# Gathering the output in two tiles of two groups by turns instead of one tile of four groups

## The chip, the cores and the metric

One core of one Trainium2 chip runs the whole program. The metric is the device time of one launch in microseconds. Three runs of the kernel before gave 1164.0, 1164.9 and 1166.22 us; the median is 1164.9 us.

## The reference

The input `x` has 4 batches of 12608 rows with 128 columns, and there are 32 inducing rows. Two attention steps follow each other (`mab`): first the inducing rows attend over all of `x` and give 32 rows `h` per batch, then every row of `x` attends over `h`. On that result stands a channel mix in the manner of RWKV: each row is mixed with the row before it, once for a key path of width 1024 and once for a gate.

```python
def mab(q, kv):
    s = scale * (q @ kv.T); a = exp(s - s.max(-1)); a /= a.sum(-1) + 1e-09
    return a @ kv
h = mab(I, x);  x = mab(x, h)
x_prev = x shifted by one row (a zero row first)
xk = mu_k * x + (1 - mu_k) * x_prev ;  xr = mu_r * x + (1 - mu_r) * x_prev
k = maximum(xk @ w_k, 0);  v = k * k @ w_v;  r = sigmoid(xr @ w_r)
return r * v            # (4, 12608, 128) float32
```

## The kernel before

**Tiles.** A batch is cut into 25 groups of 512 rows (the last has 320), and a group into 4 units; a unit is a quarter of the 1024 inner columns. The program is one long list of 400 units, written out by hand: the order in which the instructions of each engine stand is the order of the calls in the loop over `n` at the end, and no scheduler moves them.

**One unit.** `up` (L779, L781) multiplies the attention weights of the group, which lie in a tile `R`, by products `W` of `h` with the weights, 4 matmuls on TensorE (PE) into the accumulator `ps_a`. `square` takes that apart: VectorE (DVE) writes the positive part to `k_t` (L791), ScalarE (ACT) or DVE squares it into a high part `kh` (L796, L793), ACT squares it once more in full (L797), and GpSimd (POOL) takes the difference, the low part `kl` (L799). Four units later (`LAG`) `down` adds `kh`·`wvh`, `kh`·`wvl` and `kl`·`wvh` into `ps_v`, 6 matmuls (L810).

**The end of a group.** After the last unit of a group has been through `down`, `gate` multiplies by the sigmoid on DVE into `oT` (L815), and `store` transposes `oT` in blocks of 32 by 32 on DVE into the output tile `ot` (L826). `store` of group g of a batch is called at unit 4g+9 of that batch, ahead of that unit's `down` and of what is due there. `ot` has one buffer (`bufs=1`) of 4 groups. After the fourth group four DMAs, one for each 32 partitions, take it to memory (L833), 256 KB each. The next group's transpose (the first of the next four) writes the same buffer, and so it has to wait until all four have landed. The last four full groups of the last batch are stored one by one, and the group of 320 rows goes through another tile, `aT`. Before the first group the buffer of `ot` also holds the weights `wv_sb` while they are split into a high and a low part.

**Work for the next batch beside it.** `stage_a` transposes blocks of `x` on DVE (L333, from `xb` to `xs`) for the next batch, in segments of 12 units; four sets of four DMAs (L336) carry the pieces to the tiles `xt`, and 6 units after the last set is due PE multiplies them with the inducing rows (`scores`, L361). Then DVE takes the maximum (L364, L370), PE spreads it (L371), ACT takes exponentials, DVE transposes them (L405), and PE sums (L426). `stage_b` computes the attention weights of later groups, a high and a low part (`ah`, L656, and `al`, L660), and for each group a copy of one column from the group before (L593) and four DMAs (L670) put them into its `R`.

**One queue.** All these DMAs, but for three loads at the start, are issued by SyncE (SP) in the order of the calls. SP does one after the other: an entry that waits for its data holds up all that stand behind it.

Of the kernel before, what the change touches and what calls it, by code (L numbers as in the profile page):

```python
# [8 lines left out]
F32 = mybir.dt.float32  # L9
# [10 lines left out]
def kernel(  # L20
# [12 lines left out]
    B, N, C = x.shape  # L33
    M = inducing.shape[0]
    F = w_k.shape[1]
    P = 128
    Q = 4
    FC = F // P
    G = 512
    BLK = Q * G  # L40
    NBLK = (N + BLK - 1) // BLK
    TAIL = N - (NBLK - 1) * BLK
    WF = F + C
    UC = 2
    LAG = 4
    NU = FC // UC
    assert NBLK == 7 and C == P and M * Q == P and F % 1024 == 0 and TAIL % Q == 0
    scale = 1.0 / float(C) ** 0.5
# [8 lines left out]
    mp = ctx.enter_context(tc.tile_pool(name="mp", bufs=2))  # L57
# [19 lines left out]
    nc.scalar.dma_start(out=mur, in_=mu_r.rearrange("(p o) -> p o", o=1))  # L77
    wk_sb = const.tile([P, F], F32, name="wk_sb")
    wr_sb = const.tile([P, C], F32, name="wr_sb")
    wv_sb = mp.tile([P, Q * G], F32, name="ot", bufs=1)[:, :F].rearrange("p (c d) -> p c d", d=C)  # L80

    def load_weight(dst, src, n, raw):

# [666 lines left out]
    NG = (NBLK - 1) * Q + 1  # L750
    UB = NG * NU

    class Group:
# [63 lines left out]
        def store(self):  # L817

            g, w = self.g, self.w
            if g == NG - 1:  # L820
                self.S.ot = st.tile([P, G], F32, name="aT")
            elif g % Q == 0:
                self.S.ot = out_tile()
            ot = self.S.ot
            o = (g % Q) * G
            nc.vector.transpose(out=ot[:, o:o + w], in_=self.oT)  # L826
            span = 1 if self.b == B - 1 and g // Q == NBLK - 2 else Q
            if g % span == span - 1 or g == NG - 1:
                o0 = (g % Q - g % span) * G
                t0 = (g - g % span) * G  # L830
                dst = out[self.b, t0:t0 + o - o0 + w, :].rearrange("(s q) (j d) -> j q s d", q=M, d=M)
                for i in range(Q):
                    nc.sync.dma_start(out=dst[i], in_=ot[M * i:M * (i + 1), o0:o + w]  # L833
                                      .rearrange("q (s d) -> q s d", d=M))

    def out_tile():
        return mp.tile([P, Q * G], F32, name="ot", bufs=1)


    def run(th):  # L840
# [107 lines left out]
    def start():  # L948

        sc0, df0, ex0, nm0, pl0 = stage_b_head([0, 1])  # L950
        sc1, df1, ex1, nm1, pl1 = stage_b_head([2, 3])
        hi0, lo0, put0 = pl0[0]
        box = {}

        def bank():
            return pv.tile([P, G], F32, name="ps_v")

        def gate_bank(s):
            if s == 0:
                box["g"] = bank()  # L960
            return box["g"][:, s * C:(s + 1) * C]

        wa = [wpart(s, 0, bank) for s in range(2)]
        wb = [wpart(s, 1, bank) for s in range(2)]
        wg = [wpart(s, None, lambda s=s: gate_bank(s)) for s in range(2)]
        assert F // G == 2
        hi1, lo1, put1 = pl0[1]
        run([sc0, lambda: halo(batches[0], 0), df0, wa[0][0], wa[1][0], wa[0][1], ex0, wa[1][1], wa[0][2], nm0, wb[0][0], hi0, lo0, put0,
             wa[1][2], wb[0][1], hi1, lo1, wb[0][2]])
        at(0, mixed_r)  # L970
        for f in (wb[1][0], wb[1][1]):
            soon(0, f)
        for n, f in ((0, wb[1][2]), (0, sc1), (1, df1), (1, ex1), (2, nm1)):
            at(n, f)
        for prod, high, low in wg:
            at(1, prod)
        for prod, high, low in wg:
            at(1, high)
            at(2, low)
        soon(2, put1)  # L980
        for k, (high, low, put) in enumerate(pl1):
            at(k + 2, high)
            at(k + 3, low)
            at(k + 5, put)
        at(4, lambda: units[0][0].zgate(first=True))
# [16 lines left out]
    for b in range(B):  # L1002
        for g in range(NG):
            grp = Group(b, g)
            units += [(grp, u) for u in range(NU)]
    end = len(units) - 1
    late = []
    with tc.manual_schedule():
        head()
        start()  # L1010
        for n in range(len(units) + LAG + 2):
            grp, u = units[n] if n < len(units) else (None, n % NU)
            old, ou = units[n - LAG] if LAG <= n < len(units) + LAG else (None, 0)
            m = n - LAG - 1
            if 0 <= m < len(units) and units[m][1] == NU - 1:
                units[m][0].gate()
# [3 lines left out]
            else:  # L1020
# [9 lines left out]
                if n == end:  # L1030
                    run(late)
                    late = []
                if n >= NU and u == 1:
                    grp.zgate()
                if u == NU - 2 and n + 2 < len(units):
                    nxt = units[n + 2][0]
# [37 lines left out]
```

## Time and profile before

| | |
|---|---|
| median of 3 runs | 1164.9 us |
| the profiled execution | 1164.7 us |
| its span, first to last instruction | 1162.9 us |
| outside the span | 1.8 us |
| mean granted TensorE clock | 0.993 |
| PE busy | 1117.1 us |
| POOL busy | 947.7 us |
| DVE busy | 933.2 us |

All are from one profiled execution except the median. A row of the waits names the instruction that waited, what ended the wait, the total in us, how often, and the longest. A row of the timeline has the start and the duration in us, the engine (SPq is SP's queue issuing a DMA), the line, the operation, output and input, how many were merged into the row, and in brackets the idle time of that engine just before it with what ended it. The duration of an SPq row is the time in which the queue was taken up with issuing, not the transfer.

### The profile page before, as it was taken

The numbers are of one execution on the slowest core, as the hardware profiler recorded it, in microseconds if no ns is written. First come the engines' busy times: TensorE is split into PE (matmuls) and PEld (weight loads), VectorE is DVE, ScalarE is ACT, GpSimd is POOL, SyncE is SP. The second block draws the span as 40 slices with busy tenths as digits, with TensorE's granted clock in tenths as the row PEclk, the third lists the DMA queues.
The fourth block names the chain that finished last, engine by engine and source line by source line (L and its number), as shares of the span: only waits on it lengthen the run. The fifth ranks groups of instructions, "written<-read, shape, count | busy, mean of one in ns | idle before, by whom it ended". The sixth has DMA issues, their size and how long they took to land.

```text
span 1162.9 us, 17578 instructions
## 1 busy us (share of the span) xinstructions
PE 1117.1 (96%) x5746; PEld 836.6 (72%) x5746; DVE 933.2 (80%) x1259; ACT 970.9 (83%) x1107; POOL 947.7 (81%) x413
## 2 busy tenths in 40 slices
PE   6789999999999999999999999999999999999997
PEld 4466777776677777777768777677768777777886
DVE  5788888886878888888787889897787888877665
ACT  5488888887888888788978988888789888889996
POOL 1168888887787888888879888878878899999997
PEclk9999999999999999999999999999999999999999
DMA  9122654544226355465043553645204314432231
GB/s 295 42 50 64 130 120 112 102 117 81 44 56 134 105 106 123 108 133 120 5 77 77 117 124 105 133 98 122 45 18 79 63 34 73 73 64 46 43 46 34
DMA packets 273515, 102.31 MB, mean 88 GB/s; under 512 B 232816, under 2 KB 248336, under 8 KB 271120
## 3 DMA queue, kind: packets, MB, share of 16 engines
q1 hardware_dynamic: 273088, 101.17, 40.7%
q8 instruction: 46, 0.75, 0.3%
q14 instruction: 45, 0.37, 0.1%
q10 hardware_dynamic: 336, 0.02, 0.0%
HBM read 28.07 MB, written 25.82 MB: 46 GB/s over the span
## 4 chain that ended last, share of the span: by engine, by line
PE 65%; DVE 13%; ACT 8%; issue 5%; DMA 4%; SPq 4%; POOL 0%; DVEq 0%; ACTq 0%; POOLq 0%
PE ps_v L810 33%; PE ps_a L779 12%; PE ps_a L781 11%; DVE k_t L791 5%; ACT kh L796 2%; DMA out_dram<-ot 2%; PE pb_a L426 2%; ACT k_t L797 2%; PE ps_v L768 1%; SPq L833 1%; PE pb_b L616 1%; PE ps_v L769 1%; PE pb_a L361 1%; ACT L771 1%; ACT L633 1%
## 5 line engine op out<-in xcount | busy, mean ns | idle before, releaser
L799 POOL TENSOR_TENSOR kl<-k_t,kh 128x1024 fp32r<-128x1024 f32 (+2 forms) x400 | 939.0, 2375 | 175.8 <-ACT k_t L797 156.5
L791 DVE TENSOR_SCALAR k_t<-ps_a 128x1024 f32<-128x1024 f32 (+1 forms) x400 | 480.7, 1202 | 154.3 <-PE ps_a L781 143.5
L797 ACT ACTIVATE k_t<-k_t 128x1024 f32<-128x1024 f32 (+1 forms) x400 | 418.2, 1048 | 45.5 <-DVE kh L793 34.3
L796 ACT ACTIVATE kh<-k_t 128x1024 fp32r<-128x1024 f32 (+1 forms) x352 | 366.0, 1040 | 106.7 <-DVE k_t L791 56.1
L779 PE MATMUL ps_a<-R,W 128*128 128x512 f32 (+1 forms) x800 | 326.3, 408 | 6.7 <-DMA R<-al 3.4
L781 PE MATMUL ps_a<-R,W 128*128 128x512 f32 (+1 forms) x800 | 314.2, 393 | 0.0
L810 PE MATMUL ps_v<-kh,wvh 128*128 128x512 f32 (+1 forms) x800 | 252.2, 396 | 5.6 <-ACT rT L771 5.2
L810 PE MATMUL ps_v<-kh,wvl 128*128 128x512 f32 (+1 forms) x800 | 250.1, 394 | 0.0
L810 PE MATMUL ps_v<-kl,wvh 128*128 128x512 f32 (+1 forms) x800 | 250.0, 394 | 0.0
L779 PEld LDWEIGHTS ps_a<-R,W 128*128 128x128 f32 x800 | 151.4, 189 | 84.8 <-issue 20.7
L810 PEld LDWEIGHTS ps_v<-kh,wvh 128*128 128x128 f32 x800 | 147.9, 189 | 42.4 <-ACT rT L771 10.2
L810 PEld LDWEIGHTS ps_v<-kl,wvh 128*128 128x128 f32 x800 | 150.4, 189 | 35.8 <-POOL kl L799 0.3
L810 PEld LDWEIGHTS ps_v<-kh,wvl 128*128 128x128 f32 x800 | 150.3, 189 | 35.0
L781 PEld LDWEIGHTS ps_a<-R,W 128*128 128x128 f32 x800 | 151.3, 189 | 29.9
L826 DVE STREAM_TRANSPOSE ot<-oT 128x512 f32<-128x512 f32 x96 | 67.4, 702 | 12.0 <-DMA out_dram<-ot 11.2
L815 DVE TENSOR_TENSOR oT<-ps_v,rT 128x512 f32<-128x512 f32 (+1 forms) x100 | 66.6, 666 | 2.4 <-PE ps_v L810 0.2
L793 DVE SCALAR_TENSOR_TENSOR kh<-ps_a,k_t 128x1024 fp32r<-128x1024 f32 x48 | 58.8, 1225 | 5.4 <-PE ps_v L810 0.5
L771 ACT ACTIVATE rT<-ps_v 128x512 f32<-128x512 f32 (+1 forms) x99 | 57.3, 579 | 0.3
L333 DVE STREAM_TRANSPOSE xs<-xb 128x512 f32<-128x512 f32 x72 | 50.0, 694 | 1.8 <-DMA xb<-in_x_dram 1.6
L771 ACT ACT_TABLE_LOAD x31 | 39.8, 1283 | 0.6
L768 PE MATMUL ps_v<-R,W 128*128 128x512 f32 (+1 forms) x99 | 39.1, 395 | 0.1
L769 PE MATMUL ps_v<-R,W 128*128 128x512 f32 (+1 forms) x99 | 38.7, 391 | 0.0
(192 smaller groups left out, 642.3 us busy)
## 6 DMA issues: line engine op xcount, KB each, us to landing
out_dram<-ot SPq DMA_DIRECT2D x92, 256.0 KB, 4.3
xb<-in_x_dram SPq DMA_DIRECT2D x18, 1024.0 KB, 5.3
xt<-xs SPq DMA_DIRECT2D x288, 64.0 KB, 2.0
R<-ah SPq DMA_DIRECT2D x184, 64.0 KB, 2.0
R<-al SPq DMA_DIRECT2D x184, 64.0 KB, 2.0
kh<-in_x_dram SPq DMA_DIRECT2D x4, 512.0 KB, 7.0
kl<-in_x_dram SPq DMA_DIRECT2D x4, 512.0 KB, 6.3
xb<-in_x_dram SPq DMA_DIRECT2D x8, 256.0 KB, 5.5
```

Source lines behind the costliest of these rows:

```text
L768: nc.tensor.matmul(out=ps[:, :w], lhsT=S.W[0][:, F:WF], rhs=R[:, 1:w + 1], start=True, stop=False)
L771: nc.scalar.activation(out=self.rT, in_=ps[:, :w], func=AF.Sigmoid)
L779: nc.tensor.matmul(out=ps[:, c, :w], lhsT=S.W[0][:, cs], rhs=R[:, 1:w + 1], start=True, stop=False)
L781: nc.tensor.matmul(out=ps[:, c, :w], lhsT=S.W[1][:, cs], rhs=R[:, 0:w], start=False, stop=True)
L791: nc.vector.tensor_scalar(out=k, in0=self.ps[:, :, :w], scalar1=0.0, scalar2=None, op0=ALU.max)
L793: nc.vector.scalar_tensor_tensor(out=kh, in0=self.ps[:, :, :w], scalar=0.0, in1=k, op0=ALU.max, op1=ALU.mult)
L796: nc.scalar.activation(out=kh, in_=k, func=AF.Square)
L797: nc.scalar.activation(out=k, in_=k, func=AF.Square)
L799: return lambda eng, a, z: eng.tensor_tensor(out=kl[:, :, a:z], in0=k[:, :, a:z], in1=kh.bitcast(F32)[:, :, a:z], op=ALU.subtract)
L810: nc.tensor.matmul(out=self.v, lhsT=wt[:, fc, :], rhs=kk[:, c, :], start=(fc == 0 and n == 0), stop=(fc == FC - 1 and n == 2))
L815: nc.vector.tensor_tensor(out=self.oT, in0=self.v, in1=self.rT, op=ALU.mult)
L826: nc.vector.transpose(out=ot[:, o:o + w], in_=self.oT)
```

## The change

A constant `UO = 2` is added. The tile `ot` holds `UO` groups instead of four, and its pool keeps its two buffers (the pool's default), so that the bytes in SBUF stay the same. `store` takes a new tile at every even group, and issues its four DMAs after every odd group, 128 KB each instead of 256 KB. The helper `out_tile` goes away. The one-by-one stores of the last four full groups of the last batch and the last group of each batch stay as they are.

```diff
+    UO = 2
...
-    wv_sb = mp.tile([P, Q * G], F32, name="ot", bufs=1)[:, :F].rearrange("p (c d) -> p c d", d=C)
+    wv_sb = mp.tile([P, UO * G], F32, name="ot")[:, :F].rearrange("p (c d) -> p c d", d=C)
...
-            elif g % Q == 0:
-                self.S.ot = out_tile()
+            elif g % UO == 0:
+                self.S.ot = mp.tile([P, UO * G], F32, name="ot")
             ot = self.S.ot
-            o = (g % Q) * G
+            o = (g % UO) * G
             nc.vector.transpose(out=ot[:, o:o + w], in_=self.oT)
-            span = 1 if self.b == B - 1 and g // Q == NBLK - 2 else Q
+            span = 1 if self.b == B - 1 and g // Q == NBLK - 2 else UO
             if g % span == span - 1 or g == NG - 1:
-                o0 = (g % Q - g % span) * G
+                o0 = (g % UO - g % span) * G
                 t0 = (g - g % span) * G
                 dst = out[self.b, t0:t0 + o - o0 + w, :].rearrange("(s q) (j d) -> j q s d", q=M, d=M)
                 for i in range(Q):
                     nc.sync.dma_start(out=dst[i], in_=ot[M * i:M * (i + 1), o0:o + w]
                                       .rearrange("q (s d) -> q s d", d=M))
-
-    def out_tile():
-        return mp.tile([P, Q * G], F32, name="ot", bufs=1)
```

In the order of the instructions PE, DVE, ACT and POOL keep every row in its place, a row's line number apart. What differs there is what some of them wait for. The first place is DVE at the end of the fifth group of the first batch, where a transpose turns to a new output buffer; before (DMAHW0 to DMAHW7 are the eight semaphores by which DMAs report that they have landed, taken by turns; Pool, PE, Activation and DVE are those of the engines):

```order
L791 TENSOR_SCALAR k_t<-ps_a 128x1024 [waits PE_49,Pool_49]
L826 STREAM_TRANSPOSE ot<-oT 128x512 [waits DMAHW2_49,DMAHW7_49,DMAHW1_49,DMAHW0_49]
L364 TENSOR_REDUCE mx_1487<-pb_a 128x1 [waits PE_49]
L791 TENSOR_SCALAR k_t<-ps_a 128x1024 [waits PE_49,Pool_49]
L660 TENSOR_TENSOR al<-pb_b,ah 128x512 [waits DMAHW6_49,DMAHW5_49,Activation_49]
```

The same place in the changed kernel, where lines stand one further down:

```order
L792 TENSOR_SCALAR k_t<-ps_a 128x1024 [waits PE_49,Pool_49]
L827 STREAM_TRANSPOSE ot<-oT 128x512 [waits DMAHW3_49]
L365 TENSOR_REDUCE mx_1492<-pb_a 128x1 [waits PE_49]
L792 TENSOR_SCALAR k_t<-ps_a 128x1024 [waits PE_49,Pool_49]
L661 TENSOR_TENSOR al<-pb_b,ah 128x512 [waits DMAHW4_49,DMAHW3_49,DMAHW5_49,DMAHW2_49,DMAHW6_49,DMAHW1_49,Activation_49]
```

The transpose waits for the four stores of the block that has just ended before, and afterwards for a store of groups 0 and 1, whose buffer it takes over; no row has moved.

On SP the stores move. This is its queue at the start of the first batch, ahead of the attention weights of group 4, before:

```order
L336 DMA xt<-xs 32x512 x16
L205 DMA xb<-in_x_dram 128x2048
L593 DMA R<-R 128x1
L670 DMA R<-ah 32x512
L670 DMA R<-al 32x512
```

The same stretch in the changed kernel:

```order
L337 DMA xt<-xs 32x512 x16
L206 DMA xb<-in_x_dram 128x2048
L834 DMA out_dram<-ot 32x32x32 x4
L594 DMA R<-R 128x1
L671 DMA R<-ah 32x512
```

The stores of groups 0 and 1 now stand ahead of the column copy and the four DMAs that fill the `R` of group 4.

This is SP's queue in the second segment of the second batch, from the second to the third of its four sets of `xt`, before:

```order
L336 DMA xt<-xs 32x512 x4
L593 DMA R<-R 128x1
L670 DMA R<-ah 32x512
L670 DMA R<-al 32x512
L670 DMA R<-ah 32x512
L670 DMA R<-al 32x512
L336 DMA xt<-xs 32x512 x4
```

The same stretch in the changed kernel:

```order
L337 DMA xt<-xs 32x512 x4
L834 DMA out_dram<-ot 32x32x32 x4
L594 DMA R<-R 128x1
L671 DMA R<-ah 32x512
L671 DMA R<-al 32x512
L671 DMA R<-ah 32x512
L671 DMA R<-al 32x512
L337 DMA xt<-xs 32x512 x4
```

The stores of groups 0 and 1 of the second batch stand between the two sets, where no store stood before.

## The prediction

> **What bounds the kernel now.** I read the shares of the engines and the chain that ended last first:
>
> ```profile
> PE 1117.1 (96%) x5746; PEld 836.6 (72%) x5746; DVE 933.2 (80%) x1259; ACT 970.9 (83%) x1107; POOL 947.7 (81%) x413
> PE ps_v L810 33%; PE ps_a L779 12%; PE ps_a L781 11%; DVE k_t L791 5%; ACT kh L796 2%; DMA out_dram<-ot 2%; PE pb_a L426 2%; ACT k_t L797 2%; PE ps_v L768 1%; SPq L833 1%; PE pb_b L616 1%; PE ps_v L769 1%; PE pb_a L361 1%; ACT L771 1%; ACT L633 1%
> ```
>
> PE is busy for 1117.1 of 1162.9 us, so that 45.8 us of idle PE is all that any edit of waits can bring. The chain gives the stores of `ot` 2% of the span (some 23 us), but a step of that chain lasts as long as the store, while PE beside it works on. What counts is PE's idle time. The waits of DVE, which executes the transpose, and those of PE after the first 90 us:
>
> ```profile
> DVE ot L826 <- DMA out_dram<-ot: 11.2, 6, 2.7
> DVE k_t L791 <- PE ps_a L781: 143.5, 177, 2.8
> PE pb_b L371 <- DVE mx L370: 4.0, 3, 1.8
> PE ps_a L779 <- DMA R<-al: 3.4, 2, 2.1
> PE pb_b L371 <- DVE al L660: 2.2, 3, 1.1
> PE pb_a L426 <- DVE e L405: 0.7, 1, 0.7
> ```
>
> DVE loses 11.2 us to the one output buffer, in six waits. It waits 143.5 us for PE, so it has time to spare; only what PE then waits for DVE is lost. The third, fifth and sixth row name such waits. One of the places in full, the queue, DVE and PE in turn:
>
> ```profile
> 501.93 4.54 SPq L833 DMA_DIRECT2D out_dram<-ot  x4
> 510.11 0.71 DVE L826 STREAM_TRANSPOSE ot<-oT 128x512 f32<-128x512 f32 x1 [2.43 <-DMA out_dram<-ot]
> 513.18 0.38 PE L371 MATMUL pb_b<-ident,mx 128*128 128x128 f32 x1 [0.86 <-DVE al L660]
> ```
>
> The queue issues the stores of a block from 501.93 to 506.47, they land, the next transpose starts 2.43 us late at 510.11, the DVE work behind it (L364, L660) is late too, and PE stands for 0.86 us. A wait of 2.43 us costs 0.86.
>
> **What the change removes.** With two buffers the transpose waits for stores that were issued two groups earlier. A group takes about 11 us (100 groups in the span), far more than the stores need, so all six waits go. What PE gets back at the other places:
>
> ```profile
> 137.05 0.38 PE L371 MATMUL pb_b<-ident,mx 128*128 128x128 f32 x1 [0.26 <-DVE al L660]
> 225.21 0.32 PE L426 MATMUL pb_a<-xb,e 128*32 128x128 f32 x4 [0.73 <-DVE e L405]
> 790.94 0.38 PE L371 MATMUL pb_b<-ident,mx 128*128 128x128 f32 x1 [1.13 <-DVE al L660]
> 276.66 0.35 PE L371 MATMUL pb_b<-ident,mx 128*128 128x128 f32 x1 [1.80 <-DVE mx L370]
> 550.50 0.35 PE L371 MATMUL pb_b<-ident,mx 128*128 128x128 f32 x1 [1.14 <-DVE mx L370]
> 269.33 0.71 DVE L826 STREAM_TRANSPOSE ot<-oT 128x512 f32<-128x512 f32 x1 [2.00 <-DMA out_dram<-ot]
> ```
>
> With 0.86 the first three make 0.26 + 0.73 + 0.86 + 1.13 = **2.98 us**. Nothing else stands next in line there: PE's list of waits has no second releaser at these instructions.
>
> The stall at 276.66 is another matter. The same matmul waits 1.14 us in the next batch, where no store held DVE; so the store's part is not 1.80 but 1.80 - 1.14 = 0.66 us. Why the rest stays is seen in POOL and DVE:
>
> ```profile
> 274.13 2.37 POOL L799 TENSOR_TENSOR kl<-k_t,kh 128x1024 fp32r<-128x1024 f32 x1 [2.01 <-ACT k_t L797]
> 274.56 1.95 DVE L370 TENSOR_TENSOR mx<-mx,mx 128x1 f32<-128x1 f32 x1
> 549.08 1.27 DVE L370 TENSOR_TENSOR mx<-mx,mx 128x1 f32<-128x1 f32 x1
> 277.35:280.76 3.41, 3.41 (x10) 2.66 (x9) 0.94 (x4) 2.11 (x2) 1.48 (x1) 0.50 0.09 18
> 550.50:553.91 3.41, 3.41 (x16) 2.83 (x17) 2.13 (x5) 2.24 (x3) 2.41 (x1) 1.00 0.09 18
> ```
>
> An operation on 128 by 1 numbers takes 1.95 and 1.27 us, and in the first batch it ends at 276.51, where POOL's ends (276.50). It is held by whatever POOL is doing, and that is not touched by the change. The last two rows are windows of the trace (length, busy time of PE, its weight loads, DVE, ACT and POOL, then the clock): right after this stall PE ran for 3.41 us at a granted clock of 0.50, which loses 3.41 x 0.5 = 1.7 us. Behind the stall of 1.14 us in the next batch the clock is full. Without the store I expect 1.14 here too, and no halving: 0.66 + 1.7 = **2.36 us**.
>
> The Trainium skill ("TensorE: Matmul & The Clock Gate", "What's actually happening") says that the clock is halved by a monitor that looks at windows of 3413 ns that run on regardless of the program; the 3.41 us of the row agrees. By that rule it is chance in part whether a stall falls into one window, so that this term might be 0.66; the sum below would then be a gain of 4.4 instead of 6.1.
>
> **What it adds.** The stores rise from 124 DMAs to 216 (the 92 large DMAs of the first row below, 23 blocks of four groups, become 184; 16 of 64 KB and 16 of the last groups stay), at the same bytes and the same rows of 128 bytes. SP issues them, and the columns and the pieces of `R` and `xt` stand behind them. The trace has sets of four with 256 KB each and with 64 KB each, not with 128:
>
> ```profile
> out_dram<-ot SPq DMA_DIRECT2D x92, 256.0 KB, 4.3
> 406.66 4.24 SPq L833 DMA_DIRECT2D out_dram<-ot  x4
> 410.94 1.77 SPq L593 DMA_DIRECT2D R<-R  x1
> 395.31 0.51 SPq L593 DMA_DIRECT2D R<-R  x1
> 1140.16 1.94 SPq L833 DMA_DIRECT2D out_dram<-ot  x4
> ```
>
> A large set takes the queue 4.24 us and holds the next entry for 1.77 - 0.51 = 1.26 us more: 5.5. A set of 64 KB takes 1.94. A set of 128 KB lies between 1.94 and 5.5; by size, a third of the way, 1.94 + 3.56 / 3 = 3.1 us. I take 3.1, since issuing grows with size in these rows. Two sets then take 6.2 where one took 5.5: in sum almost nothing, but each half stands elsewhere. Where a large set stood the queue is 2.4 us earlier, and where none stood it is 3.1 us later. Two places gain and two lose.
>
> *Gain, `xt` in the fourth segments.* The scores take 1.06 us where nothing holds them, as in the row at 405.82 below; two took longer:
>
> ```profile
> 454.89 4.39 SPq L833 DMA_DIRECT2D out_dram<-ot  x4
> 470.09 2.64 SPq L336 DMA_DIRECT2D xt<-xs  x4
> 473.18 2.11 PE L361 MATMUL pb_a<-xt,indT 128*32 128x512 f32 x8
> 750.85 1.90 PE L361 MATMUL pb_a<-xt,indT 128*32 128x512 f32 x8
> 399.53 2.43 SPq L336 DMA_DIRECT2D xt<-xs  x4
> 405.82 1.06 PE L361 MATMUL pb_a<-xt,indT 128*32 128x512 f32 x8
> 674.71 3.24 SPq L336 DMA_DIRECT2D xt<-xs  x4
> 683.42 1.06 PE L361 MATMUL pb_a<-xt,indT 128*32 128x512 f32 x8
> xt<-xs SPq DMA_DIRECT2D x288, 64.0 KB, 2.0
> ```
>
> The last of the four `xt` DMAs from 470.09 is issued at about 472.2 and lands 2.0 us later, when the scores have begun. They lose 2.11 - 1.06 = 1.05 us, and 0.84 at 750.85. The queue had been late since the large set at 454.89; 2.4 us earlier, both losses go: **1.89 us**.
>
> *Loss, `xt` in the second segments.* The set from 399.53 has its last DMA issued at 399.53 + 3 x 0.62 = 401.4; it lands at 403.4, 2.4 us ahead of its use at 405.82. With 3.1 us more ahead of it PE waits **0.7 us**. Below 2.4 us the set is hidden, at 5.5 it costs 3.1. Its twin in the third batch, issued by 677.95 at the latest, lands by 679.95, 3.5 us ahead of its use at 683.42, and stays hidden.
>
> *Loss, the first `R`.*
>
> ```profile
> 96.61 0.70 DVE L826 STREAM_TRANSPOSE ot<-oT 128x512 f32<-128x512 f32 x1
> 98.21 0.52 SPq L670 DMA_DIRECT2D R<-ah  x1
> 101.25 0.51 SPq L670 DMA_DIRECT2D R<-al  x1
> 104.56 0.47 PE L779 MATMUL ps_a<-R,W 128*128 128x512 f32 x1 [1.31 <-DMA R<-al]
> ```
>
> PE waits here for the `R` of group 4 already. Its first high part went out at 98.21 and the low part at 101.25, when DVE had it. Now the queue first waits for group 1's transpose (97.31), and is free of the stores at 97.4 + 3.1 = 100.5; column and high part take 0.51 + 0.52 and two gaps, so the low part goes at 101.65: **0.4 us** late. At 1.94 it is hidden; at 5.5 it is 2.8 late. All other `R` are filled well ahead or behind a set that shrinks.
>
> Everything else is nothing: `wv_sb` gets a tile that group 2 takes over long after the weights were split, and the stores that end the last batch are the same.
>
> **The sum.** 2.98 + 2.36 + 1.89 - 0.7 - 0.4 = 6.1 us. The profiled execution took 1164.7 us (span 1162.9 and 1.8 outside), 0.2 below the median 1164.9. 1164.7 - 6.1 = **1158.6 us**.
>
> **The rivals.** *PE gets little of it.* DVE's time is gained, but the halved clock comes back at another stall, L361 stays late for reasons of its own, and only the four direct stalls go: 2.98 - 0.7 - 0.4 = 1.9 us, **1162.8 us**. For it: of DVE's 11.2 us the most is hidden as it is, and the three waits for L370 depend on where POOL is. Against it: each term has its own row with its own releaser.
>
> *Slower: the stores of half the size take the queue as long as the whole ones.* If a set of 128 KB takes 5.5 us, the second segment loses 3.1, the first `R` 2.8, and its stall of 1.31 + 2.8 = 4.1 brings a halved clock, 1.7: 7.6 in all. L361 gets no relief, so the gain is 5.34: 1164.7 + 2.3 = **1167.0 us**. It decides from about 4.9 us a set on. For it: in the large set three DMAs of four take over 1 us each. Against it: 64 KB takes 0.49 each. The Trainium skill ("DMA: Bandwidth & Descriptors", "Rules for kernel authors") speaks against the change here: many small transfers should be gathered into a large one, and under 64 KB one pays mostly overhead. At 128 KB the rule is not broken outright, and no row of this size is there to hold against it.
>
> *The change doesn't take the waits away.* The order of the instructions shows that the transpose now waits for a store of the pair before the last; so this is left at nothing.
>
> **How the numbers follow.** Forecast 0.78, little gained 0.16, slower 0.06. About 0.2% (2.3 us) is what a measurement of this kernel can tell from no change: faster is below 1162.6. The forecast's own bounds: with sets of 1.94 us both losses vanish (1157.5), and one of the three stalls before L370, or one halved clock more or less, moves it by up to 1.7 to either side: 1155.8 to 1161.4. With little gained the range reaches up to 1163.0. So 1155.8 to 1163.0, faster 0.78, same 0.16, slower 0.06.
>
> **What would show it.** In the profile after: no row of L826 waiting for a store; L371 no longer waiting for L660; the stall before L371 in the first batch near 1.1 us and full clock behind it; 216 stores in sets that take some 2 to 3 us; L361 at 1.06 us in the fourth segments, and a new wait of under 1 us in the second segment of the second batch. The forecast is wrong if PE's busy time and span stay apart by the same 45.8 us, if a halved clock shows at a new place, or if the sets take over 4.9 us.

## The result and the profile after

The changed kernel takes 1156.13 us (median of 6 runs, 1155.37 to 1159.7) where the kernel before takes 1164.45 us on the same chip (6 runs, 1162.18 to 1166.22). The ratio is 0.9936, with a 95% interval of 0.9918 to 0.9954: 8.3 us faster. The forecast was faster, by 6.1 us, to 1158.6 us; the time lies in the range, close to its lower end. The profiled execution took 1155.37 us with a span of 1153.6, that is 9.3 us less span than before.

The shares of the engines and the chain that ended last, after:

```profile
PE 1111.2 (96%) x5746; PEld 834.2 (72%) x5746; DVE 933.7 (81%) x1259; ACT 971.4 (84%) x1107; POOL 948.4 (82%) x413
PE 75%; DVE 11%; ACT 8%; issue 4%; DMA 1%; SPq 0%; DVEq 0%; ACTq 0%
```

The engines do the same work as before in a shorter span, and the step `out_dram<-ot`, 2% of the chain before, is down to a single one of 2.23 us. PE's busy time is 5.9 us less for the same instructions: its rows last longer in a stretch at half clock, of which this execution has fewer (below), and a row that waits inside, as the scores did, counts as busy. The waits of DVE and PE that answer to those of before; a row has the total, how often, and the longest:

```profile
DVE k_t L792 <- PE ps_a L782: 140.6, 180, 2.2
PE ps_a L780 <- DMA R<-al: 3.6, 2, 2.3
PE pb_b L372 <- DVE mx L371: 3.4, 3, 1.1
```

There is no row of L827 (L826 before) waiting for a store, none of PE waiting at L372 for L661 and none of PE waiting for L405. What is left is the wait for the maximum, three times 1.1 us, and the two for `R`. The place that the prediction showed in full, in the second batch, in SP's queue, DVE and PE:

```profile
495.95 2.48 SPq L834 DMA_DIRECT2D out_dram<-ot  x4
501.42 0.70 DVE L827 STREAM_TRANSPOSE ot<-oT 128x512 f32<-128x512 f32 x1
505.98 0.38 PE L372 MATMUL pb_b<-ident,mx 128*128 128x128 f32 x2
```

The rows of DVE and PE carry no bracket any more. The stores of 128 KB have left the queue at 498.43, and a store lands 2.7 us after its issue (4.3 with 256 KB), so that even a transpose into the same buffer would have found it free, at 501.1. That is the first hint that the second buffer is not what matters.

The places where the prediction expected a gain and a loss from the queue, the scores in the fourth segments and in the second segment of the second batch, with what stands in the queue ahead of them:

```profile
395.47 2.44 SPq L337 DMA_DIRECT2D xt<-xs  x4
428.89 2.48 SPq L834 DMA_DIRECT2D out_dram<-ot  x4
450.26 2.49 SPq L834 DMA_DIRECT2D out_dram<-ot  x4
461.83 2.44 SPq L337 DMA_DIRECT2D xt<-xs  x4
468.58 2.89 SPq L834 DMA_DIRECT2D out_dram<-ot  x4
```

```profile
400.91 1.07 PE L362 MATMUL pb_a<-xt,indT 128*32 128x512 f32 x8
468.03 1.06 PE L362 MATMUL pb_a<-xt,indT 128*32 128x512 f32 x8
743.49 1.07 PE L362 MATMUL pb_a<-xt,indT 128*32 128x512 f32 x8
```

All three take their undisturbed 1.06 or 1.07 us: both gains came, and the loss did not. Only the second half of the block (450.26) stands where the whole one stood, with one `xt` set between it and that of 461.83; its first half left at 428.89, and the stores of 468.58 are the first half of the next block, issued behind the last `xt` set. The 46 sets of 128 KB took the queue 2.25 to 3.59 us, 2.48 in the middle; the 23 whole ones before took 4.05 to 5.05, 4.39 in the middle. I had estimated 3.1 for the half ones.

The stall before the maximum in the first batch, the wait for the first `R` of the second batch, and the stretches of 3.41 us behind both (length, busy time of PE, PEld, DVE, ACT and POOL, the clock, the DMA share and GB/s):

```profile
273.43 0.46 PE L372 MATMUL pb_b<-ident,mx 128*128 128x128 f32 x2 [1.12 <-DVE mx L371]
339.99 0.47 PE L780 MATMUL ps_a<-R,W 128*128 128x512 f32 x1 [2.29 <-DMA R<-al]
```

```profile
273.43:276.84 3.41, 3.41 (x16) 2.83 (x17) 2.14 (x5) 2.25 (x3) 2.42 (x1) 1.00 0.02 4
341.37:344.78 3.41, 3.41 (x11) 2.92 (x10) 2.22 (x3) 2.12 (x2) 1.36 (x1) 0.50 0.35 77
```

The first stall fell from 1.80 to 1.12 us and the clock behind it is full, as forecast; the second is as before, with its halved clock. The first `R`, where I expected 0.4 us of loss:

```profile
96.15 2.29 SPq L834 DMA_DIRECT2D out_dram<-ot  x4
...
100.07 0.51 SPq L671 DMA_DIRECT2D R<-al  x1
```

```profile
103.43 0.47 PE L780 MATMUL ps_a<-R,W 128*128 128x512 f32 x1 [1.36 <-DMA R<-al]
```

1.36 us stands where 1.31 stood: nothing lost that counts.

To see where 9.3 us went I took, in both traces, the distance from the start of each matmul to the start of the next, less the usual distance of that pair of matmuls, and summed it by the place at which the matmul came late, from the eighth unit on. The levels also hold small regular delays; what counts is the difference.

| place | before | after | change | forecast |
|---|---|---|---|---|
| up to the eighth unit | 81.3 | 80.1 | -1.2 | 0 |
| scores (L361) | 9.6 | 7.7 | -1.9 | -1.89 and +0.7 |
| maximum (L371) and L426 | 18.6 | 13.7 | -4.9 | -3.64 |
| halved clock | 2.6 | 1.2 | -1.4 | -1.7 |
| late `R` (L779) | 5.1 | 5.4 | +0.3 | +0.4 |

The rest, in small pieces, is about half a us, and behind the last matmul after has 0.3 us more. The 1.2 us at the start belong to the clock, not to the change:

```profile
55.46:58.87 3.41, 3.41 (x14) 1.61 (x16) 2.83 (x5) 0.61 (x3) 0.00 (x0) 0.50 0.00 0
65.70:69.10 3.40, 3.40 (x10) 2.62 (x9) 3.24 (x7) 2.13 (x4) 2.31 (x2) 0.50 0.02 5
```

These are two stretches at half clock in the trace of before; after has only one there, at 64.90. The first two kernels of the experiments begin as the kernel before does, and their profiled executions reach the eighth unit at 80.0 and 81.2 us, with no such stretch and with two. The profiled executions of two kernels below (one buffer with half stores, and four tiles of one) spend 2 us more than before up to the eighth unit, at a mean clock of 0.992 and 0.991.

### The profile page after: what moved, and what is told of

The parts are those of the page before. It is cut to its first block, busy times and chain, and to the rows that moved or that the text cites. A ratio compares the mean times of both kernels' runs of the same rounds, so it can differ in the third digit from the quotient of the medians.

```text
span 1153.6 us, 17710 instructions
## 1 busy us (share of the span) xinstructions
PE 1111.2 (96%) x5746; PEld 834.2 (72%) x5746; DVE 933.7 (81%) x1259; ACT 971.4 (84%) x1107; POOL 948.4 (82%) x413
## 4 chain that ended last, share of the span: by engine, by line
PE 75%; DVE 11%; ACT 8%; issue 4%; DMA 1%; SPq 0%; DVEq 0%; ACTq 0%
PE ps_v L811 38%; PE ps_a L780 14%; PE ps_a L782 12%; DVE k_t L792 4%; ACT kh L797 2%; PE pb_a L427 2%; PE pb_b L617 2%; PE ps_v L769 2%; PE ps_v L770 2%; PE pb_a L362 2%; ACT k_t L798 1%; ACT L772 1%; ACT L634 1%; DVE oT L816 1%; DVE kh L794 1%
## 5 line engine op out<-in xcount | busy, mean ns | idle before, releaser
L827 DVE STREAM_TRANSPOSE ot<-oT 128x512 f32<-128x512 f32 x96 | 67.4, 702 | 0.0
```

## The experiments

My theory after the result: PE's gain comes from two sources, the wait of the transpose for its buffer, and the queue of SP, in which a whole set takes 4.4 us and the `xt` pieces stand behind it. Each is worth about what the table says. The rivals: all comes from the buffer; or all comes from the size of the sets, and the second buffer does nothing.

**The wait gone, the queue kept.** The first group of each four goes to a tile of its own, so that its transpose finds a free buffer; the stores still leave together after the fourth group, as four DMAs of 64 KB and four of 192 KB. Edit of the kernel before (its core):

```diff
-            elif g % Q == 0:
-                self.S.ot = out_tile()
...
+            if g == NG - 1 or (g % Q == 0 and not alone):
+                self.S.of = st.tile([P, G], F32, name="aT")
...
+            elif g % Q == Q - 1:
+                pieces = [(self.S.of, 0, g - 3, G), (self.S.ot, G, g - 2, 3 * G)]
```

> The buffer wait alone is taken away: the first group of four goes to the tile aT, the other three to the one tile ot, and all are stored after the fourth group, as before (eight stores at that place instead of four, 64 KB and 192 KB each, estimated at about the 5.5 us of queue time that a block takes before). My sum holds term by term: PE gets back the direct stalls (2.98 us) and the stall of the first batch with its halved clock (2.36), not the scores of the fourth segments (1.89). So about 5.3 us below before, 1159, L826 without waits for stores, L361 still near 2 us at two places. Rival, that the split of the queue's stores is what counts: no change, 1164.5. Rival, that the buffer wait is all: as the changed kernel, 1156.

Measured 1162.84 us against 1164.67 of before, ratio 0.9989 (0.9977 to 1.0001): almost nothing of the expected gain. The waits that are left, and the queue at the fourth segment of the second batch:

```profile
DVE aT L823 <- DMA out_dram<-aT: 5.5, 2, 3.4
PE pb_a L361 <- DMA xt<-xs: 1.8, 2, 1.3
```

```profile
453.76 2.24 SPq L841 DMA_DIRECT2D out_dram<-aT  x4
456.10 3.02 SPq L841 DMA_DIRECT2D out_dram<-ot  x4
459.16 1.35 SPq L593 DMA_DIRECT2D R<-R  x1
```

Of DVE's 11.2 us of waits 5.5 are left, twice, and those are of this experiment's own making: the group of 320 rows uses the tile `aT` too. The queue was taken up for 5.3 us by the eight stores, longer than by a whole set, and PE's scores now wait for `xt` with a row of their own. By the table's measure the scores are 4.8 us worse than before (14.4 against 9.6). So this kernel is not clean; the next leaves the queue alone.

**The wait alone gone.** The transpose of the first group of each four is simply called one unit (2.3 us) later, when its buffer is free; the stores and their places in the queue stay untouched.

```diff
-            if 1 <= m <= len(units) and units[m - 1][1] == NU - 1:
-                units[m - 1][0].store()
+            for back in (1, 2):
+                if back <= m < len(units) + back and units[m - back][1] == NU - 1:
+                    done = units[m - back][0]
+                    if (done.g % Q == 0 and done.g < NG - 1) == (back == 2):
+                        done.store()
```

> The kernel before with one move: the first transpose of each four is called one unit (some 2.5 us) later; tile, stores and the queue's order stay. The longest wait was 2.67 us, so nearly all of them go, and nothing of the queue is touched. My sum: the direct stalls of 2.98 us and the 2.36 of the first batch go, the scores of the fourth segments stay near 2 us: 5.3 below before, 1159 to 1160. Rival, that the queue is the whole cause: no change. Rival, that the wait is the whole gain: 1156.5.

Measured 1163.59 us against 1164.32, ratio 0.9993 (0.9982 to 1.0005): no change, against an expected gain of 4 to 5 us. What is left of the transpose's wait is one of 0.3 us, and PE waits at L371 for L660, five times and little:

```profile
DVE ot L826 <- DMA out_dram<-ot: 0.3, 1, 0.3
PE pb_b L371 <- DVE al L660: 1.2, 5, 0.3
```

The halved clock behind the maximum of the first batch is gone too, and of the direct stalls about half (2.4 of 4.9 us by the table's measure; the moved transpose now stands ahead of L660). This execution also has no halved clock behind the first `R` of the second batch, where before has one; the later transpose does not account for that. Now the scores at the three places where they stand behind a whole set; first the kernel before (the rows of 473.18 and 750.85 are in the prediction), then this one:

```profile
234.22 1.06 PE L361 MATMUL pb_a<-xt,indT 128*32 128x512 f32 x8
```

```profile
233.49 2.67 PE L361 MATMUL pb_a<-xt,indT 128*32 128x512 f32 x8
470.99 2.82 PE L361 MATMUL pb_a<-xt,indT 128*32 128x512 f32 x8
749.83 2.72 PE L361 MATMUL pb_a<-xt,indT 128*32 128x512 f32 x8 [0.16 <-PE ps_v L810]
```

The last pair tells it best. PE comes to the scores at 749.83, 1.02 us sooner than before (750.85), and leaves them at 752.55, where before left them at 752.75: 0.82 of the 1.02 us are given back on the spot. At 233.49 PE comes 0.73 us sooner and ends 0.88 later, since a whole set took 5.92 us here (5.05 at most before), which the later transpose does not explain. At 470.99 it comes 2.19 us sooner and still ends 1.48 sooner, so that not all is given back there. By the table's measure the scores lose 3.9 us more than before, the direct stalls 2.4 less. The queue that PE waits for:

```profile
450.26 2.44 SPq L336 DMA_DIRECT2D xt<-xs  x4
452.79 4.42 SPq L833 DMA_DIRECT2D out_dram<-ot  x4
457.26 1.79 SPq L593 DMA_DIRECT2D R<-R  x1
...
467.61 3.65 SPq L336 DMA_DIRECT2D xt<-xs  x4
```

With the rows between them, SP issues from 450.26 to 471.26 with no gap over 0.2 us. The last `xt` DMA leaves shortly before 471.26 and lands 2 us later; scores that begin at 470.99 must wait. A PE that is no longer held by the transpose is held by the queue. The gains of the two reliefs aren't two separate sums: without the second, nothing of the first can be measured (the interval leaves room for 2.1 us at most). Two tests are missing: two whole buffers with whole stores, and a relieved queue with the wait kept. So how the 8.3 us divide between the two reliefs stays open.

**One buffer, half stores.** The tile stays one of four groups with one buffer, only the stores leave after every second group.

```diff
-            span = 1 if self.b == B - 1 and g // Q == NBLK - 2 else Q
+            span = 1 if self.b == B - 1 and g // Q == NBLK - 2 else 2
```

> The one tile of four groups stays, and only the stores are made after every second group. Then the first transpose of the next four waits for four stores of 128 KB instead of 256: by the trace of after they take the queue 2.3 instead of 4.2 us and land in 2.7 instead of 4.3, so that the last one lands 3.4 us earlier, and the longest wait before was 2.67. My theory now: all waits go without a second buffer, and the kernel is as fast as the changed one, 1156 to 1157. Rival, that the second buffer is what does it: waits of L826 stay near 11 us in sum, only the scores of the fourth segments gain, 1162.5.

Measured 1156.53 us, ratio 0.9937 (0.9923 to 0.995): the whole gain of the change by one number, with one buffer. The list of DVE's waits has no row of `ot` either: the last half of a block needs 2.5 us of the queue and lands in 2.8, where the whole needed 4.4 and 4.3, so it is there about 3.4 us sooner, more than the longest wait of before (2.7).

**One tile of two groups.** The change with half the memory: a single buffer of two groups, which each pair of groups takes over from the last (the same at the line of `wv_sb`).

```diff
-                self.S.ot = mp.tile([P, UO * G], F32, name="ot")
+                self.S.ot = mp.tile([P, UO * G], F32, name="ot", bufs=1)
```

> One tile of two groups instead of two, everything else as in the changed kernel; each second transpose now waits for the stores of the pair that has just ended. By the trace of after such a set lands at least 0.2 us before the next transpose at nearly every place (one place 0.7 us too late). My theory: hardly any wait, within 1 us of the changed kernel, 1156 to 1157. Rival, that the second buffer is needed: twice as many turns as before, waits of over 10 us in sum, 1161 or more.

Measured 1155.31 us, ratio 0.9922 (0.991 to 0.9934), not to be told apart from the change. Its trace has just two waits of L827 for a store:

```profile
DVE ot L827 <- DMA out_dram<-ot: 0.9, 2, 0.4
```

So the second buffer, the visible part of the change, brings nothing here; the smaller sets bring it all.

**Four tiles of one group**, with stores of 64 KB after every group (`UO = 1`, four buffers; the weights `wv_sb` lie in two of them at the start):

```diff
-    UO = 2
+    UO = 1
...
-                self.S.ot = mp.tile([P, UO * G], F32, name="ot")
+                self.S.ot = mp.tile([P, G], F32, name="ot", bufs=4)
```

> Four tiles of one group by turns in the same space, stores of 64 KB after every group (400 instead of 216). Sets of 64 KB take the queue 1.94 us, four of them 7.8 per four groups instead of 4.8. By the room that the pieces of xt have left (1.0 us and more at the tightest) it is hidden nearly everywhere: 1156 to 1158. Rival, that the number of stores has a price of its own in the queue: the scores L361 wait in most segments, 1159 or more.

Measured 1156.4 us, ratio 0.9939 (0.9927 to 0.9951). Quarters are as good as halves and no better: 2.20 us a set in the middle (1.94 to 4.08), so twice the sets take 4.4 where a half set takes 2.5, but they are spread out, and nothing waits for them at a place that counts.

**The stores doubled.** To see what the "slower" rival would have been worth: after each half set the same data go a second time, to a spare piece of memory that nobody reads, so that a set takes the queue about twice as long.

```diff
+                if span > 1 and g < NG - 1:
+                    more = spare.tile([UO * G, C], F32, name="more")
...
+                        nc.sync.dma_start(out=dst[i], in_=ot[M * i:M * (i + 1), o0:o + w]
```

> The changed kernel, with each set of 128 KB followed by a second set of the same data to spare memory: a pair now takes the queue near 5 us, as in the rival that came out slower. The pieces of xt have some 1.6 us of room where a set stands ahead, the second set costs 2.3 to 2.7: about eight scores lose near a microsecond each, the first R loses over 2 and its stall halves the clock once more (1.7): 10 us over the changed kernel, 1166, slower than before. Rival, that the queue has room enough and only the transpose's wait counted: 1157.

Measured 1199.39 us, ratio 1.0312 (1.0289 to 1.0334): slower by 35 us, where I expected 2. The queue and the waits of PE and DVE:

```profile
447.70 2.48 SPq L835 DMA_DIRECT2D out_dram<-ot  x4
450.23 2.60 SPq L841 DMA_DIRECT2D more<-ot  x4
452.93 0.66 SPq L207 DMA_DIRECT2D xb<-in_x_dram  x1
```

```profile
PE ps_v L770 <- DVE oT L817: 16.6, 6, 4.1
PE ps_a L781 <- DMA R<-al: 6.0, 2, 3.9
PE pb_a L363 <- DMA xt<-xs: 3.6, 3, 1.6
```

```profile
DVE xs L335 <- DMA R<-al: 10.0, 3, 4.1
DVE xs L335 <- DMA xb<-in_x_dram: 10.0, 2, 5.5
DVE xs L335 <- DMA xt<-xs: 5.1, 2, 4.5
461.25 0.71 DVE L335 STREAM_TRANSPOSE xs<-xb 128x512 f32<-128x512 f32 x1 [5.52 <-DMA xb<-in_x_dram]
```

The places that I had counted, `xt` and `R`, show up with 9.6 us. The largest loss is one that I had not counted at all: the transposes of `x` on DVE (L335). They stop DVE for 25.1 us, PE waits 16.6 us for the gate product `oT` behind them, and the halved clock, 10.0 us by the table's measure against 1.2, follows. For 5.1 us of the 25.1 their tile `xs` is still waiting to be sent. The other 20.0 us, five waits, end within 0.2 us of the landing of the next block of `x` (`xb`), also the three that the list puts down to `R`. Its load stands in the queue behind the doubled stores: the one of 452.93 landed at 461.13, and DVE began at 461.25. In these five places the load took 6.3 to 8.2 us from issue to landing, 5.5 in the middle in the changed kernel. So the second copy also slows transfers, and this run does not tell the queue's share from that of the doubled traffic. There is a limit, and it isn't far: with two such sets in place of one the loss against the changed kernel is 43 us, five times the gain of the change.

**The maximum with one tensor.** The largest stall left before L372 is the wait for L371, a maximum of 128 by 1 numbers that takes 1.27 us. The prediction held that it is held by POOL. The same maximum, with the second operand as a scalar per partition:

```diff
-                nc.vector.tensor_tensor(out=L["mx"], in0=L["mx"], in1=L["mxt"], op=ALU.max)
+                nc.vector.tensor_scalar(out=L["mx"], in0=L["mx"], scalar1=L["mxt"], scalar2=None, op0=ALU.max)
```

> The changed kernel with another form of the one operation that was held by POOL (L370 of before): the maximum of two 128 by 1 numbers as a tensor with a scalar from a tile instead of two tensors. If it is held because it reads two tensors from SBUF, it takes some 0.2 us instead of 1.3, and the stalls of 1.1 us before L371 go in three batches: 3.4 us below the changed kernel, 1152.5 to 1153.5. Rival, that it waits for its data or is held in any form: 1156.

Measured 1152.02 us, ratio 0.9899 (0.9882 to 0.9916). DVE and POOL in the changed kernel, and then in this one:

```profile
272.01 1.27 DVE L371 TENSOR_TENSOR mx<-mx,mx 128x1 f32<-128x1 f32 x1
270.88 2.38 POOL L800 TENSOR_TENSOR kl<-k_t,kh 128x1024 fp32r<-128x1024 f32 x1 [1.17 <-ACT k_t L798]
```

```profile
274.32 0.20 DVE L371 TENSOR_SCALAR mx<-mx,mx 128x1 f32<-128x1 f32 x1
273.19 2.40 POOL L800 TENSOR_TENSOR kl<-k_t,kh 128x1024 fp32r<-128x1024 f32 x1 [1.19 <-ACT k_t L798]
```

With two tensors the maximum ends at 273.28, with POOL's operation (273.26); with one tensor and a scalar it takes 0.20 us in the middle of POOL's. The three stalls are gone, 3.2 us by the table's measure (4.1 to 0.9). The Trainium skill ("SBUF — State Buffer", "Who interferes with whom") has this rule: an operation of VectorE with two inputs in SBUF contends with one of GpSimd that reads SBUF, and one with at most one input there, outside the modes that use both ports, does not. These rows agree (1.27 us to POOL's end, and 0.20 beside it), for a column of one number per partition.

**Both savings of code and memory.** One tile of two groups, and the maximum with one tensor; the edit is the last two together.

> One tile of two groups (no second buffer) together with the other form of the maximum. If both hold for themselves they add: 3.4 us below the kernel with one tile of two groups, 1152. If the earlier PE only moves the stall to the next late thing: 1155.

Measured 1152.52 us, ratio 0.9901 (0.9885 to 0.9918), as the last, with half the output buffer.

**The first weights earlier.** With the maximum out of the way the wait for `R` at the start of the second batch is the longest. The weights of that group are asked for one unit earlier:

```diff
-            stage_b(b + 1, 0, at, s + 13)
+            stage_b(b + 1, 0, at, s + (12 if b == 0 else 13))
```

> The kernel with the one-operand maximum, with the attention weights of the second batch's first group asked for one unit (2.3 us) earlier; nothing of the stores is touched. If the wait for the first `R` of the second batch (2.1 to 2.3 us) and the stretch at half clock behind it (3.41 us, worth 1.7) are what is left there, both go and the time falls by up to 4 us, to 1148 to 1150 us. Rival: the chain ahead of the weights (scores, maximum, exponentials) is late as well and the same unit then waits for it, or the weights' work on VectorE now delays something else: 1152 us, no change.

Measured 1150.63 us (1149.01 to 1152.52), ratio 0.9896 (0.9873 to 0.9919), the fastest of all in the median, but its interval covers that of the kernel without this step, so the 1.4 us between them are not shown. In its trace the step is clear:

```profile
336.31 0.47 PE L780 MATMUL ps_a<-R,W 128*128 128x512 f32 x1 [0.88 <-DMA R<-al]
```

```profile
336.31:339.72 3.41, 3.41 (x17) 2.95 (x18) 2.26 (x4) 2.38 (x4) 3.41 (x3) 1.00 0.28 61
```

The wait fell from 2.29 to 0.88 us and the clock behind it is full. A halved stretch need not be in every execution, so that in the median it can be worth less than the 1.7 us of a single one. The kernel with both savings shows it: there PE waited 2.28 us for the same `R`, and no halved clock came.

```profile
339.62 0.47 PE L780 MATMUL ps_a<-R,W 128*128 128x512 f32 x1 [2.28 <-DMA R<-al]
```

```profile
339.40:342.80 3.40, 3.18 (x16) 2.79 (x17) 1.90 (x3) 1.00 (x2) 2.98 (x2) 1.00 0.31 67
```

## Why the prediction was right, and where its steps were not

- **The six waits of the transpose go, and the stalls of PE behind them.** Right. 2.98 + 0.66 = 3.64 us were forecast at L371 and L426, 4.9 came. Part of the difference is how a row shows a stall: a matmul is shown with some 0.39 us while the next may start 0.23 us after it, so the bracket leaves out up to 0.16 us of each; four stalls make 0.6. Another 0.42 us stood before two matmuls of L426, late by 0.20 us at 464.1 and 0.22 at 741.8 before and on time after, which no row of the waits shows. The remaining 0.2 to 0.3 us I can't place.
- **The stall before the maximum of the first batch falls to that of the others, and the clock stays whole.** Right: 1.12 us and 1.00. The halved clock gave 1.4 us between these two executions, 1.7 were forecast. As the last experiment shows, the same stall of 2.3 us is followed by a halved clock in one execution and not in another, so this term is one of chances. Ten of the eleven traces have a stall of 2.1 to 2.6 us at that `R`; seven have the halved clock there, three do not. The rule of free-running windows that the prediction cites from the Trainium skill ("TensorE: Matmul & The Clock Gate", "What's actually happening") would have it so, and these traces agree.
- **The scores of the fourth segments lose their delay.** Right to the size: 1.9 us.
- **A loss of 0.7 us in the second segment and of 0.4 us at the first `R`.** Wrong, both from one term: 3.1 us for a half set, by a third of the way from a small set to a whole one. It is 2.48 in the middle, 2.29 at the first `R`, so that the 0.4 us were within what I had put on too much. In the second segment the half set did come between: the fourth `xt` set started 6.29 us ahead of the scores before (399.53 to 405.82) and 5.44 now (395.47 to 400.91). Of its margin of 2.4 us 0.85 went, not 3.1, because the queue came to that segment less late than before: its second set started 19.25 us ahead of the scores before (386.57) and 20.49 now (380.42).
- **The sum.** 8.3 us by the medians instead of 6.1: the two losses that didn't come are 1.1, direct stalls larger than their brackets 1.3. Profile against profile it is 9.3, with 1.2 us of clock in the first 80 us that are not the change's. One premise of the sum was too narrow: the 45.8 us of idle PE are not all that an edit of waits can bring. Idle PE is 42.4 us after, only 3.4 less; the other 5.9 us came out of PE's busy time. And the upper bound of the forecast alone doesn't follow from its terms: 1158.6 + 1.7 is 1160.3, not 1161.4.
- **The price of each part was put at the wrong door.** The prediction gave 2.98 + 0.66 us, most of its gain, to the second buffer ("With two buffers the transpose waits for stores that were issued two groups earlier"), and added the queue's 1.89 to it. The runs show that one buffer does as well (1156.53 and 1155.31 us), and that taking the wait away alone gives nothing that can be measured (1163.59 and 1162.84 us, against 1164.32 and 1164.67). The common cause of the transpose's wait and of the late `xt` is the whole set: 4.4 us in the queue, 1.2 us more held up behind it, and 4.3 us until it has landed. That the sum came out near all the same is luck as far as this division goes: the change relieves both at once, so that an error in the shares didn't show in the total.
- **The rival "PE gets little of it"** was wrong for this change, and came closer for the change that I believed to be looking at: with the wait alone gone 0.7 us are left, not shown to differ from nothing. That rival had L361 stay late and 1.9 us gained; that the gain is given back at L361 it did not say.
- **The rival "slower"** had its mechanism and its deciding point (about 4.9 us a set) in sight, and the sets stayed well below it. Its price of 2.3 us over the time before was not tested by itself. Stores of twice the number and bytes cost 35 us over it: the rival counted two places, while such stores also hold up the loads of `x` and with them DVE. The rule of the Trainium skill that spoke against the change ("DMA: Bandwidth & Descriptors", "Rules for kernel authors", to gather many small transfers into a large one) did not decide here: two half sets take the queue 2 x 2.48 = 4.96 us, a whole one 4.39 and some 1.2 of delay behind it, so splitting cost nothing in sum, and it let `xt` pass between the halves.

## What to carry to other kernels

When a wait for a buffer and a late transfer on the same queue show up side by side, look first for the large entry in that queue that causes both: cutting it in two can be worth more than another buffer, and it costs no memory. Don't add up the idle time of one engine behind two such causes: take away one alone in an experiment, since the engine may only arrive earlier at the next wait. And before a queue gets more to do, look for stretches in which it issues without a gap, and for loads that stand behind them: in the run with doubled stores the loss was not the sum of a few late places.

## What the runs showed of the hardware

- A set of four stores in rows of 128 bytes takes SP's queue 4.39 us at 256 KB each, 3.1 at 192 KB, 2.48 at 128 KB and 1.94 to 2.2 at 64 KB, and lands 4.3, 3.8, 2.7 and 1.9 us after issue (medians). Where a copy of one column came next, it took 1.3 to 2.9 us behind a whole set, 1.8 in the middle, instead of 0.5; behind half a set it took 0.6.
- A maximum of one number per partition took 0.20 us with a scalar per partition as second operand, and 1.27 to 1.95 us with two tensors while POOL worked on an operation of its own; it then ended with POOL's.
- After the same wait of 2.3 us PE ran at half clock for 3.41 us in one execution and at full clock in another. In the eleven traces, between 85 us and the end of the program, most stalls of PE of 1.80 us and more came with such a stretch, three did not, and none of 1.63 us or less did. The times of one kernel, 1155.37 to 1159.7 us after the change, are spread by about as much as two or three such stretches (1.7 us each) make.
